# A new fixed order of all units in an attention backward kernel, placed with a longer latency for GpSimd's loads

## The chip, the cores and the metric

The kernel runs on one core of one Trainium2 chip. The metric is the device time of one execution in microseconds (us), lower is better. A profile shows a single execution.

## The reference, cut to what matters

```python
def _fwd_reference(q, k, v):                 # q: 32 x 32 x 4 x 128, k and v: 32 x 4 x 2048 x 128, bf16
    rep = Hq // Hkv                          # 8 query heads share one K/V head
    k = jnp.repeat(k, rep, axis=1)
    v = jnp.repeat(v, rep, axis=1)
    scores = jnp.einsum("bhqd,bhkd->bhqk", q, k) * D ** -0.5
    p = _softmax(scores, axis=-1)
    return jnp.einsum("bhqk,bhkd->bhqd", p, v)

def reference(q, k, v, grad_out):
    _out, _vjp = jax.vjp(_f, q, k, v)
    return (_out, *_vjp(grad_out))           # out, dq, dk, dv
```

There are 32 batches. A batch reads 4 MiB of K and V and writes 4 MiB of dK and dV; q, grad_out, out and dq are 32 KB each.

## The kernel before

The work of a batch is cut into units (a load, a group of eight transposes, a group of matmuls, a copy out of PSUM, a store). Five tables of constants decide everything else: `PLACE` and `SHIFT` give each unit a modelled time, and units are emitted in the order of these times; `ENGINE` and `SWAP` say which of ScalarE and VectorE empties a PSUM bank; `BANK` says which bank a unit gets. The order is fixed when the program is built. At run time each engine, and each DMA queue, takes its instructions in that order, and waits in front of one whose inputs or buffers are not ready.

```python
CAP = dict(q=4, k=8, v=4, ..., out=6)         # buffers: K tiles, V tiles, output tiles of 1 MiB, ...
PERIOD = 21.3
PLACE = dict(LQ=[-48.2636], LK=[-18.0693, -12.8344], LV=[-1.1987, -0.6906], ...)
SHIFT = {0: dict(...), 1: dict(...), ..., -1: dict(LQ=[49.6961], ...)}   # first and last batches

def plan(n_batches):
    # ... [cut]
            u.at = b * PERIOD + PLACE[name][i] + (SHIFT[special][name][i] if special in SHIFT else 0.0)
    # ... [cut]
    return sorted(order, key=lambda u: u.at), bank_of

def emit(u):
    # ... [cut]
        if name == "LQ":                                        # loads of q and grad_out, by GpSimd
            nc.gpsimd.dma_start(out=t["q"][:], in_=q_r[b])
            nc.gpsimd.dma_start(out=t["go"][:], in_=go_r[b])
        elif name in ("LK", "LV"):                              # 1 MiB: K or V of two heads, SyncE's queue
            # ... [cut]
                nc.sync.dma_start(out=whole[:, h], in_=src[b, g][:, h])
        elif name == "dop":                                     # grad_out / l, four GpSimd instructions
            # ... [cut]
                nc.gpsimd.tensor_scalar(out=t["dop"][r, h % 2, :], in0=t["go"][r, :], scalar1=t["rinv"][r, :],
                                        scalar2=None, op0=ALU.mult)
        elif name in ("DVs", "DKs"):                            # 1 MiB: dV or dK of two heads, SyncE's queue
            nc.sync.dma_start(out=(dv_r if name == "DVs" else dk_r)[b, g], in_=...)
```

Below, `31:LQ` is unit LQ of batch 31 (the last one), `0:DVs` the dV stores of batch 0. `DVh` and `DKh` are the half-size stores that the last batch uses instead of `DVs` and `DKs`.

Of the kernel before, what the change touches and what calls it, by code (L numbers as in the profile page):

```python
# [25 lines left out]
    LQ=[-48.2636], LK=[-18.0693, -12.8344], LV=[-1.1987, -0.6906], QT=[-8.9345], QTe=[-8.0517], KT=[3.2794, 2.2075,  # L26
    7.1287, 2.9279, -5.1008, 3.9474, 1.1495, 6.9051], KTe=[4.4019, 3.316, 7.8294, 3.9376, -3.2033, 4.9456, 1.413,
    8.201], VT=[10.6087, 11.8661, 12.1333, 11.0016, 22.6693, 19.1402, 21.0035, 29.0087], VTe=[11.5263, 13.3348,
    13.3464, 11.5339, 25.2055, 20.4113, 22.6987, 29.4066], S=[8.9164, 9.1359, 10.1684, 10.2742], MX=[9.726, 11.188],
    EX=[11.5488, 12.7509], L=[13.5403], dop=[14.9237], qp=[15.0712], rs=[22.4217], ET=[12.8706, 15.3517],  # L30
    ETe=[13.759, 16.5487], DT=[33.7403, 33.874], DTe=[35.0099, 35.0323], O=[16.8199, 17.0848, 17.1211, 17.3327],
    Oe=[17.6328], Os=[99.048], DQ=[49.0977, 49.2643, 51.8834, 52.2176], DQe=[52.222], DQs=[124.1403], DL=[18.4003],
    qfree=[30.7856], ofree=[101.8924], rfree=[76.464], DP=[19.5657, 19.5918, 32.7696, 32.8363], DS=[20.4794,
    33.0602], DV=[16.5613, 18.6959, 20.5469, 23.6255], DVe=[19.153, 18.3782, 19.7253, 19.9101, 21.6161, 22.5498,
    24.3354, 25.3252], DVs=[39.3395, 39.4734], DVh=[387.3484, 385.4967, 324.0755, 340.9939], DK=[27.2708, 29.0136,
    35.1757, 36.4881], DKe=[27.6123, 28.7618, 32.2561, 29.9139, 35.424, 36.2058, 37.166, 37.6438], DKs=[48.8067,
    50.1041], DKh=[309.6939, 275.5323, 368.4023, 239.5107], gfree=[72.3], dfree=[80.3411], vfree=[33.6388, 31.3008],
    efree=[38.0449], dsfree=[63.0633])
ENGINE = dict(
    QTe="A", KTe="DADAAAAA", VTe="ADDADAAD", ETe="AA", DTe="AD", Oe="D", DQe="A", DVe="AAADADAD", DKe="ADAAADAD")  # L40
SHIFT = {
    0: dict(
        LQ=[-644.2765], LK=[-547.0453, -364.6817], LV=[-242.4579, -342.359], QT=[-632.7948], QTe=[-537.9094],
        KT=[-526.8631, -326.7945, -226.1179, -229.4531, -211.8817, -445.3626, -187.0175, -311.721], KTe=[-449.298,
        -165.5918, -147.4492, -161.5852, -132.9361, -215.7495, -111.6072, -147.4306], VT=[-97.4249, -92.3852,
        -107.2125, -59.3954, -4.7301, -90.5139, -47.2652, -2.9351], VTe=[-60.891, -41.3598, -100.4245, -33.8442,
        -5.7782, -35.7373, -46.6873, -2.5874], S=[-133.3945, -128.0896, -116.6589, -105.6517], MX=[-103.1307,
        -96.1978], EX=[-80.1859, -76.7809], L=[-69.1857], dop=[-39.1633], qp=[-3.0986], rs=[-28.5145], ET=[-62.3285,
        -40.4913], ETe=[-61.4401, -37.8095], DT=[-2.4503, 3.8768], DTe=[-3.2726, 5.1407], O=[-34.6895, -34.5605,
        -32.5426, -26.7439], Oe=[-22.3532], Os=[-90.6858], DQ=[0.9913, 1.1827, -0.1837, -0.4072], DQe=[0.4358],  # L50
        DQs=[-25.8332], DL=[-23.0407], qfree=[3.6845], ofree=[-77.4158], rfree=[-47.2796], DP=[-15.6901, -15.0886,
        -0.2677, -0.1337], DS=[-9.2259, 0.0507], DV=[-20.5882, -20.1317, -17.8862, -7.8066], DVe=[-22.7759, -19.3155,
        -14.5522, -18.4952, -14.7281, -14.851, -6.2499, -2.6803], DVs=[-7.1188, -6.2006], DVh=[95.9489, -13.6628,
        190.2837, 256.3967], DK=[-2.3257, 0.2661, -0.196, 4.6202], DKe=[-1.4443, -2.8552, -2.3906, 0.6497, 4.8007,
        4.4534, 5.2752, 5.067], DKs=[2.5501, 6.7883], DKh=[92.5601, 315.3518, 14.3092, 206.3769], gfree=[-33.114],
        dfree=[12.6331], vfree=[2.3226, -3.4381], efree=[16.241], dsfree=[-14.3615]),
    1: dict(
        LQ=[-273.2258], LK=[-172.9572, -173.197], LV=[-143.8962, -84.7141], QT=[-102.2987], QTe=[-95.0311],
        KT=[-13.5143, -10.931, -12.2749, 1.5848, -41.1927, -6.8878, -4.2267, -0.3856], KTe=[-14.2854, -7.3948,
        -5.0963, 3.5831, -26.9748, -1.8969, 2.7732, 0.0956], VT=[-0.92, 9.5148, 7.5599, 0.4076, 9.5424, -1.3453,  # L60
        7.2294, 3.2881], VTe=[-1.2694, 8.8214, 8.208, 4.7262, 7.0746, -0.1221, 7.2436, 4.0334], S=[-0.4612, 0.1422,
        -0.8601, -0.7784], MX=[-0.0261, -0.3402], EX=[-0.3014, -1.4823], L=[2.9579], dop=[5.4261], qp=[8.1163],
        rs=[18.2432], ET=[4.2204, 4.2313], ETe=[5.5073, 3.7202], DT=[10.4883, 9.0141], DTe=[12.2528, 8.8384],
        O=[4.7696, 4.6756, 4.6399, 4.8799], Oe=[5.2421], Os=[-65.6303], DQ=[1.38, 2.4818, 0.5752, 0.4214],
        DQe=[0.8305], DQs=[-55.6573], DL=[6.6664], qfree=[-4.54], ofree=[-57.6955], rfree=[-31.2509], DP=[6.481,
        7.1462, 1.8519, 2.011], DS=[6.8437, 2.1623], DV=[6.1219, 4.2673, 4.013, 2.3696], DVe=[3.5646, 4.7633, 4.6339,
        3.2794, 4.2827, 2.5896, 2.6562, 2.5872], DVs=[-2.2225, -1.6614], DVh=[-48.0565, 92.0837, 212.991, 35.3116],
        DK=[1.4616, 2.399, 1.9843, 3.2316], DKe=[2.8105, 2.4108, 0.0521, 1.7291, 2.7773, 2.093, 4.3314, 3.6258],
        DKs=[-0.2539, 3.2382], DKh=[166.0226, -179.6575, -73.4159, 147.7363], gfree=[-20.4604], dfree=[-2.9502],
        vfree=[-0.986, 9.6916], efree=[9.973], dsfree=[-2.5173]),  # L70
    2: dict(
        LQ=[-226.2607], LK=[-125.0715, -101.8322], LV=[-0.0207, 5.1438], QT=[8.3657], QTe=[8.4261], KT=[-0.6224,
        0.899, -0.6109, 1.3692, -3.2051, 0.6568, -5.266, -0.6214], KTe=[-0.8606, 0.1636, 0.71, 0.4623, -3.8052,
        1.5449, -3.7401, 2.1648], VT=[4.6333, 1.8901, 0.9838, 3.0692, 0.7141, -0.2386, 5.2825, 2.8587], VTe=[6.9543,
        2.3385, 0.1001, 3.5582, -0.6809, -0.0455, 7.0247, 2.6881], S=[0.7118, 0.7725, 0.9176, 1.9061], MX=[1.3006,
        1.0295], EX=[2.6275, 2.1271], L=[1.7013], dop=[4.1629], qp=[6.121], rs=[26.8258], ET=[1.7596, 0.7913],
        ETe=[0.9226, 1.8347], DT=[0.0306, 1.0605], DTe=[-0.3559, 0.5948], O=[-0.6169, -0.689, 1.3759, 2.5991],
        Oe=[2.9753], Os=[-67.6709], DQ=[0.0477, 0.0266, 0.0798, 0.0503], DQe=[0.8654], DQs=[-29.5725], DL=[2.9999],
        qfree=[4.1668], ofree=[-15.8956], rfree=[8.5061], DP=[2.2626, 2.4079, -0.183, 0.2604], DS=[1.8788, 0.8895],
        DV=[3.9405, 2.0583, 1.9364, 0.8421], DVe=[2.3675, 2.5347, 1.8823, 1.7249, 0.973, 0.3188, 1.0135, 0.1142],  # L80
        DVs=[2.2247, 2.1669], DVh=[89.449, -133.5564, 149.9551, -67.7309], DK=[0.4886, 0.4113, 0.2255, -0.6123],
        DKe=[1.0637, 0.5283, -1.1784, 1.4927, 0.3966, -0.1425, -0.8541, -0.295], DKs=[0.0017, -0.7345],
        DKh=[-24.8477, -236.2928, 68.0068, -87.7762], gfree=[-8.276], dfree=[-24.2037], vfree=[7.272, 7.4296],
        efree=[0.4751], dsfree=[-3.0715]),
    -4: dict(
        LQ=[15.7312], LK=[9.1388, 3.5298], LV=[2.6948, 4.1417], QT=[4.5533], QTe=[5.4834], KT=[3.5433, 2.5662,
        -0.2541, 0.1587, 3.1776, -0.1333, -0.521, -6.2674], KTe=[2.8804, 1.5709, -0.1428, 0.5823, 2.6427, 0.1147,
        1.0893, -3.6722], VT=[0.4775, 1.6209, 0.0714, 0.8068, 1.8141, -4.6081, -1.7901, -1.974], VTe=[-0.3763,
        0.4613, -0.2881, 0.6884, 2.0307, -4.2152, -2.3562, -2.0356], S=[-0.7909, -0.605, -0.0342, 0.0555],
        MX=[1.4859, 0.26], EX=[0.4082, -0.1924], L=[0.2697], dop=[0.4758], qp=[1.2736], rs=[29.0407], ET=[1.3562,  # L90
        -1.1711], ETe=[1.0688, -1.0541], DT=[0.2943, 0.7101], DTe=[-0.2636, 0.009], O=[-1.5808, -0.9766, -0.8997,
        0.289], Oe=[0.9255], Os=[123.0701], DQ=[2.6734, 3.7048, 2.5956, 3.0928], DQe=[5.0872], DQs=[-3.9513],
# [48 lines left out]
        vfree=[366.8082, 177.2502], efree=[412.9433], dsfree=[391.0614])}  # L141
SWAP = {
    0: dict(
        KTe="-xx-x---", VTe="--x-x-x-", DTe="-x", DQe="x", DVe="x-xx----", DKe="xx--xx--"),
    1: dict(
        QTe="x", KTe="x-x-x-x-", VTe="-xxxx---", DTe="-x", DVe="-x--xx-x", DKe="xx--xxxx"),
    2: dict(
# [388 lines left out]
```

## Time and profile before

| | before |
|---|---|
| median of 3 executions | 694.3 us (693.08 to 694.78) |
| span of the profiled execution | 691.9 us |
| moved | 274.5 MB at a mean of 397 GB/s |
| PE busy, ScalarE busy | 90%, 87% |

These lines are from the page of the kernel before. The digits are the busy share, in tenths, of 40 equal slices of the span.

```profile
span 691.9 us, 28403 instructions
...
PE   5899999999999999999999999999999998998895
...
DMA  8999999999999999999999999999999999999958
...
DMA packets 75005, 274.47 MB, mean 397 GB/s; under 512 B 6272, under 2 KB 6272, under 8 KB 74880
```

The DMA engines are busy in nearly every slice, and so is PE. The transfers have slack at the end. These are the windows of the kernel before there (first the stretch; then the busy time of PE, of its weight loads, of VectorE, ScalarE and GpSimd, with instruction counts; then the granted TensorE clock, the DMA share and GB/s):

```profile
650.00:655.00 5.00, 2.54 (x45) 1.43 (x34) 1.68 (x5) 2.13 (x5) 3.33 (x7) 0.83 0.99 395
655.00:660.00 5.00, 5.00 (x71) 3.64 (x70) 4.18 (x4) 3.50 (x6) 0.00 (x0) 0.83 0.19 74
660.00:665.00 5.00, 4.14 (x69) 2.31 (x70) 4.19 (x5) 4.77 (x7) 0.00 (x0) 1.00 0.98 385
665.00:670.00 5.00, 4.89 (x125) 3.96 (x121) 4.74 (x10) 4.81 (x8) 1.02 (x2) 1.00 0.18 63
...
685.00:692.00 7.00, 0.91 (x48) 0.56 (x40) 0.06 (x1) 1.09 (x3) 1.06 (x2) 0.91 0.55 205
```

PE has a hole in 650 to 655, and the DMA engines have holes in 655 to 660 and 665 to 670. The timelines say why. PE (start, duration, instruction, idle time before it and what ended it), then GpSimd, of the kernel before:

```profile
650.26 0.62 PE L382 MATMUL psum<-ident,k_sb 128*128 128x128 bf16 x8
653.20 0.28 PE L371 MATMUL psum<-ident,q_sb 128*128 128x128 bf16 x1 [2.33 <-DMA q_sb<-in_q_dram]
...
653.84 1.03 PE L487 MATMUL psum<-dop_sb_102,e_sb 64*128 64x256 bf16 x8
```

```profile
647.52 0.59 POOL L357 DMA_DIRECT2D q_sb<-in_q_dram  x1
648.11 0.54 POOL L359 DMA_DIRECT2D go_sb<-in_grad_out_dram  x1
...
687.12 1.06 POOL L463 DMA_DIRECT2D out_dram<-dq_sb  x2 [10.94 <-ACT dq_sb L459]
```

GpSimd issues the last loads of q and grad_out at 647.5 and 648.1 us, behind the products of batch 30. PE waits 2.33 us for q, and the groups after the wait take 1.03 us instead of 0.61. The last dq stores are issued at 687.12 us.

This is the transfer rate from 25 to 65 us, in slices of one microsecond, of the kernel before:

```profile
GB/s 397 395 410 408 307 395 399 406 397 238 262 422 389 422 406 430 410 434 410 328 332 397 408 440 389 412 397 424 410 434 406 422 389 426 418 422 422 418 406 406
```

There are dips at 29, at 34 and 35, and at 44 and 45 us.

### The profile page before, as it was taken

Reading aid. Unit: us, or ns where it says so; the run is one execution under the profiler, and the core shown is the slowest. Engines: PE = TensorE matmul, PEld = TensorE weight load, DVE = VectorE, ACT = ScalarE, POOL = GpSimd, SP = SyncE. Lnnn points to the kernel's source line nnn. Section 1 sums busy time; section 2 is a strip of 40 time slices with the busy share of each in tenths; the row PEclk is TensorE's granted clock in tenths of the full one; section 3 lists DMA queues with packets and bytes.
Section 4 is the critical chain, followed back from the end, with each engine's and each line's share of the span. In section 5 each row is a group of like instructions: output and inputs, shape, how many; then the busy total and the mean of one; then the engine's idle time right before and its main releaser. Section 6 shows DMA issues by size and latency. Waiting matters only on the chain.

```text
span 691.9 us, 28403 instructions
## 1 busy us (share of the span) xinstructions
PE 625.0 (90%) x12352; PEld 468.6 (68%) x12352; DVE 556.6 (80%) x773; ACT 599.6 (87%) x924; POOL 203.2 (29%) x426
## 2 busy tenths in 40 slices
PE   5899999999999999999999999999999998998895
PEld 4677677777777777767767666676676776766563
DVE  2788888888889888888887878778787887889685
ACT  2889988899999999998889898888988998897685
POOL 2432311333322233331133321233312333213421
PEclk9999999999999999999999999999999999999999
DMA  8999999999999999999999999999999999999958
GB/s 340 394 391 415 415 413 411 413 413 416 414 416 416 414 415 411 387 410 412 411 399 410 411 409 412 406 397 401 399 406 408 402 406 402 411 391 392 364 211 302
DMA packets 75005, 274.47 MB, mean 397 GB/s; under 512 B 6272, under 2 KB 6272, under 8 KB 74880
## 3 DMA queue, kind: packets, MB, share of 16 engines
q1 hardware_dynamic: 70784, 268.45, 97.2%
q0 software_dynamic: 4096, 4.20, 1.8%
q8 instruction: 96, 1.57, 0.8%
q14 instruction: 29, 0.24, 0.1%
HBM read 136.31 MB, written 136.31 MB: 394 GB/s over the span
## 4 chain that ended last, share of the span: by engine, by line
DMA 41%; PE 26%; ACT 21%; issue 5%; DVE 3%; POOL 3%; ACTq 0%; POOLq 0%; DVEq 0%
DMA v_sb<-in_v_dram 37%; PE psum L382 15%; PE psum L487 7%; ACT dk_sb L493 6%; ACT dv_sb L493 5%; ACT e_sb L409 4%; DMA k_sb<-in_k_dram 3%; ACT vt_sb L347 3%; PE psum L452 2%; PE psum L393 2%; DMA go_sb<-in_grad_out_dram 2%; POOL dop_sb_103 L421 1%; ACT et_sb L347 1%; POOL dop_sb_102 L421 1%; ACT kt_sb L347 1%
## 5 line engine op out<-in xcount | busy, mean ns | idle before, releaser
L493 ACT CAST dv_sb<-psum 128x1024 bf16<-128x1024 f32 x155 | 151.5, 1018 | 33.3 <-PE psum L487 30.9
L493 ACT CAST dk_sb<-psum 128x1024 bf16<-128x1024 f32 x159 | 159.1, 1022 | 21.6 <-PE psum L487 21.1
L382 PE MATMUL psum<-ident,v_sb 128*128 128x128 bf16 x2048 | 150.2, 220 | 11.4 <-DMA v_sb<-in_v_dram 7.9
L382 PEld LDWEIGHTS <-v_sb 128*128 128x128 bf16 x2048 | 118.2, 98 | 51.0 <-issue 37.4
L382 PE MATMUL psum<-ident,k_sb 128*128 128x128 bf16 x2048 | 142.3, 221 | 1.3 <-ACT dv_sb L493 0.6
L382 PEld LDWEIGHTS <-k_sb 128*128 128x128 bf16 x2048 | 119.8, 99 | 15.7 <-issue 12.5
L493 DVE CAST dv_sb<-psum 128x1024 bf16<-128x1024 f32 x101 | 122.7, 1220 | 9.2 <-PE psum L487 7.9
L493 DVE CAST dk_sb<-psum 128x1024 bf16<-128x1024 f32 x97 | 116.1, 1220 | 16.2 <-DMA out_dram<-dv_sb 9.2
L347 ACT COPY kt_sb<-psum 128x512 f32<-128x512 f32 x187 | 106.7, 612 | 4.7 <-PE psum L382 4.7
L421 POOL TENSOR_SCALAR dop_sb_103<-go_sb,rinv 32x128 bf16<-32x128 bf16 x64 | 38.4, 600 | 227.5 <-DVE rinv L414 100.0
L421 POOL TENSOR_SCALAR dop_sb_102<-go_sb,rinv 32x128 bf16<-32x128 bf16 x64 | 38.4, 600 | 227.4 <-DVE rinv L414 114.1
L473 DVE SCALAR_TENSOR_TENSOR ds_sb<-psum,delta,e_sb 128x1024 bf16<-128x1024 f32 x64 | 81.9, 1279 | 16.7 <-ACT vt_sb L347 12.1
L347 ACT COPY vt_sb<-psum 128x512 f32<-128x512 f32 x137 | 80.5, 599 | 12.1 <-PE psum L382 11.8
L350 DVE COPY vt_sb<-psum 128x1024 bf16<-128x1024 bf16 x119 | 78.7, 680 | 1.0 <-PE psum L382 1.0
L487 PEld LDWEIGHTS <-e_sb 64*128 64x128 bf16 x1024 | 50.5, 94 | 37.3 <-issue 19.0
L409 ACT ACTIVATE e_sb<-psum,m 128x1024 bf16<-128x1024 f32 x64 | 70.9, 1116 | 2.7 <-DVE kt_sb L400 2.5
L350 DVE COPY kt_sb<-psum 128x1024 bf16<-128x1024 bf16 x69 | 47.1, 683 | 17.0 <-PE psum L382 16.8
L487 PEld LDWEIGHTS <-ds_sb 64*128 64x128 bf16 x1024 | 43.2, 94 | 24.8 <-issue 10.0
L441 PE MATMUL psum<-ident,e_sb 128*128 128x128 bf16 x512 | 38.8, 219 | 11.8 <-ACT dk_sb L493 10.5
L487 PE MATMUL psum<-dop_sb_103,e_sb 64*128 64x256 bf16 x512 | 46.0, 271 | 3.6 <-POOL dop_sb_103 L421 1.2
L487 PE MATMUL psum<-dop_sb_102,e_sb 64*128 64x256 bf16 x512 | 45.9, 273 | 3.6 <-ACT dv_sb L493 0.7
L400 DVE TENSOR_SCALAR_CACHE_REDUCE kt_sb<-psum 128x1024 bf16<-128x1024 f32 x32 | 39.2, 1224 | 9.1 <-PE psum L393 8.3
(83 smaller groups left out, 757.8 us busy)
## 6 DMA issues: line engine op xcount, KB each, us to landing
k_sb<-in_k_dram SPq DMA_DIRECT2D x62, 1024.0 KB, 18.6
v_sb<-in_v_dram SPq DMA_DIRECT2D x62, 1024.0 KB, 19.7
out_dram<-dv_sb SPq DMA_DIRECT2D x62, 1024.0 KB, 18.8
out_dram<-dk_sb SPq DMA_DIRECT2D x62, 1024.0 KB, 18.8
k_sb<-in_k_dram SPq DMA_DIRECT2D x4, 512.0 KB, 5.4
v_sb<-in_v_dram SPq DMA_DIRECT2D x4, 512.0 KB, 9.7
out_dram<-dv_sb SPq DMA_DIRECT2D x4, 512.0 KB, 5.6
out_dram<-dk_sb SPq DMA_DIRECT2D x4, 512.0 KB, 4.4
```

Of the source, the lines that this page charges most:

```text
L347: nc.scalar.copy(out=out.rearrange("p c d -> p (c d)").bitcast(FP32), in_=in_.rearrange("p c d -> p (c d)").bitcast(FP32))
L350: nc.vector.tensor_copy(out=out, in_=in_)
L382: nc.tensor.transpose(out=ps[:, j, :], in_=t[x, h][:, 8 * i + j, :], identity=ident[:])
L393: nc.tensor.matmul(t[name, i][r, QW * w:QW * w + QW], lhsT=t["qdt"][:, side, r], rhs=t[x, h, i][:, CPQ * w:CPQ * w + CPQ, :], start=True, ...
L400: nc.vector.tensor_scalar(out=spent, in0=t["S", i][:], scalar1=-scale, scalar2=t["m"][:] if i else None, op0=ALU.mult, op1=ALU.min, accum_ ...
L409: nc.scalar.activation(out=t["e"][:, 2 * QW * i:2 * QW * i + 2 * QW], in_=t["S", i][:], func=ACT.Exp, bias=t["m"][:], scale=scale, accum_o ...
L421: nc.gpsimd.tensor_scalar(out=t["dop"][r, h % 2, :], in0=t["go"][r, :], scalar1=t["rinv"][r, :], scalar2=None, op0=ALU.mult)
L441: nc.tensor.transpose(out=ps[:, j, :], in_=src[:, P * c:P * c + P], identity=ident[:])
L452: nc.tensor.matmul(t[name][r, 0:D], lhsT=t[xt, c // 8][:, c % 8, r], rhs=t[x, h][:, c, :], start=(c == 0), stop=(c == C - 1), tile_positio ...
L473: nc.vector.scalar_tensor_tensor(out=t["ds"][:, w], in0=t["DP", i][:], scalar=t["dl"][:], in1=t["e"][:, w], op0=ALU.subtract, op1=ALU.mult)
L487: nc.tensor.matmul(accs[g][:, 2 * P * j:2 * P * j + 2 * P], lhsT=t[lhs][r, P * c:P * c + P], rhs=t[rhs][r, :, :].rearrange("p h d -> p (h ...
L493: copy(out=t[name[:2], "out", g][:, :, CPQ * i:CPQ * i + CPQ, :], in_=t[name[:2], i][g][:].rearrange("p (c h d) -> p h c d", h=2, d=D))
```

## The change

The intent is a better fixed order, found with a model in which a load that GpSimd issues takes longer to arrive. All five tables are replaced; no line of code that emits an instruction is changed. Its core (of 277 lines of diff; everything cut is table entries):

```diff
 PLACE = dict(
-    LQ=[-48.2636], LK=[-18.0693, -12.8344], LV=[-1.1987, -0.6906], QT=[-8.9345], QTe=[-8.0517], KT=[3.2794, 2.2075,
+    LQ=[-47.936], LK=[-16.977, -14.467], LV=[3.599, 0.95], QT=[-7.484], QTe=[-6.947], KT=[2.869, 1.617, 7.32, 1.994,
 ... [cut]
 SHIFT = {
     0: dict(
-        LQ=[-644.2765], LK=[-547.0453, -364.6817], LV=[-242.4579, -342.359], QT=[-632.7948], QTe=[-537.9094],
+        LQ=[-769.808], LK=[-539.258, -428.322], LV=[-315.151, -320.416], QT=[-617.88], QTe=[-553.295], KT=[-481.834,
 ... [cut]
     -1: dict(
-        LQ=[49.6961], LK=[15.2382, -8.4226], LV=[48.932, 13.4729], QT=[23.4499], QTe=[23.5399], KT=[21.9244, 23.1949,
+        LQ=[53.318], LK=[12.855, 10.423], LV=[-0.474, 0.666], QT=[35.277], QTe=[36.759], KT=[27.228, 18.475, 11.67,
 ... [cut: the rest of PLACE and SHIFT, one entry of ENGINE, SWAP, BANK]
```

Both programs have the same 3,936 units, the same bytes and the same sizes of transfers. What moves, read from the order of instructions:

- Steady batches: the two V loads change places in SyncE's queue; PE's order is nearly the same.
- Tail, GpSimd: before, `29:dop 29:qp 25:DQs 30:dop 31:LQ 30:qp` (among others); after, `31:LQ` comes before `25:DQs 30:dop`. On PE the transposes of the last q come later in the order.
- Head, SyncE's queue: before, `... 2:LK 1:LV | 0:DVs 0:DVs 2:LV 3:LK 2:LV 3:LK`; after, `... 2:LK 1:LV 3:LK | 0:DVs 3:LK 0:DVs 2:LV 2:LV`. One K load of batch 3 passes both first stores, the other passes one of them.

## The prediction

> What bounds the kernel now. The page's DMA row is at 9 tenths in nearly every slice: 274.5 MB at a mean of 397 GB/s over 691.9 us. By windows: the DMA engines are full (share 1.0) from about 5 us to 655 us; the rate is 412 to 416 GB/s from 100 to 260 us and 399 to 410 after. Up to about 278 us the chain of waits runs through PE and ScalarE pieces, with a period near 20.3 us a batch; from 278 to 640 us it runs through loads of v_sb, about 21.1 us apart. Wherever the transfers are the limit, reordering the engines' work gains nothing, because bytes, transfer sizes and the steady queue order stay as they are (the listing of instruction order shows only that the two V loads of a batch change places).
>
> The end is different. From 640 to 692 us the chain has no bulk load. The DMA share falls to 0.19 in 655-660, 0.18 in 665-670, 0.76 in 670-675 and 0.55 in 685-692: some 12.5 us of empty DMA time. In the same stretch PE is busy 90% or more except in 650-655 (2.54 of 5 us), where ScalarE and VectorE fall to about 2 us too. The timeline shows why: GpSimd issues the last batch's q and grad_out loads only at 647.5 and 648.1, behind the four products of batch 30 (644.8-647.5). grad_out takes 5.46 us in the chain; PE waits for q_sb until 653.2 (idle 2.33 us) and for grad_out 0.32 us on weight load; all PE work behind stands in order. The next three PE groups then take 1.03 us instead of 0.61 (granted clock 0.83 in 650-660).
>
> What the change does. No operation is added or removed: 3,936 units in both; ScalarE gets 856 units instead of 859, VectorE 648 instead of 645; a steady batch has 27 and 20 in both. The function bodies are the same. On GpSimd the last q/grad_out load moves before batch 30's products, to just after batch 29's (about 622-629 us), over 15 us ahead of its use. So the PE stall (2.3 + 0.3 us) and the slow clock after it (3 x 0.42 us) go: about 4 us, all on the chain, since the following stores wait for that PE work. The Trainium skill ("TensorE: Matmul & The Clock Gate", "Part 1") says an idle PE falls to a slower clock and must be busy about 3.4 us to regain it; the trace agrees in kind (1.03 against 0.61 us).
> Smaller things: the first K transpose no longer shares a PSUM bank with the q transpose (0.35 us, hidden behind the transfers); the last dq store is no longer ahead of the previous batch's (-0.5 us), but one transpose of dS stands closer to its use (+0.4). Head: one or two more K loads ahead of the first stores, under 1 us.
>
> Estimate: 694.3 - 4.3 = 690.0 us; range 683.5 to 694.5. Floor, from the rates: 9.2 MB moved after 655 us at the 363 GB/s that stores alone reach would end near 681 us, so over 2% (below 680.4) needs a faster middle too. Chances: faster 0.05, same 0.93, slower 0.02.
>
> Right if: no PE wait for q_sb near 650; granted clock 1.0 in 650-660; DMA share in 655-660 rises from 0.19 to about 0.6; the last dv stores start about 4 us earlier; the stretch 100-600 us keeps its rate within 1%.
>
> Wrong if: the steady rate shifts between the 416 and the 404 GB/s regimes at another time (12 us at most), or the new tail order makes a new stall (PSUM banks are all reassigned), or the end was held by the store rate alone.

## The result, and the profile after

A ratio is the mean time of one kernel's fast runs over that of the other's of the same rounds, so it is not quite the ratio of the medians quoted.

| run of the changed kernel | median (range), us | before, same rounds | ratio (95% interval) |
|---|---|---|---|
| first | 692.02 (690.35 to 695.77) | 694.34 | 0.9979 (0.995 to 1.0009) |
| `after_again` | 692.27 (690.99 to 695.29) | 694.78 | 0.9969 (0.9945 to 0.9992) |
| `after_3` | 692.14 (691.42 to 694.93) | 695.26 | 0.9962 (0.9945 to 0.9979) |
| `after_4` | 692.11 (691.4 to 695.02) | 694.66 | 0.9965 (0.9949 to 0.9982) |

The mean of the four ratios is 0.9969: the change saves about 2.2 us of 694.6, half of the 4.3 us predicted. The time is inside the predicted range, which says little, since the range (683.5 to 694.5 us) also holds the 694.3 us of the kernel before; and "within 2%" came true.

These windows of the changed kernel answer to those shown of before:

```profile
650.00:655.00 5.00, 5.00 (x79) 3.46 (x72) 4.75 (x5) 4.82 (x8) 0.00 (x0) 1.00 0.96 386
655.00:660.00 5.00, 3.05 (x64) 1.70 (x65) 3.35 (x6) 3.65 (x6) 0.00 (x0) 1.00 0.90 361
660.00:665.00 5.00, 5.00 (x123) 4.14 (x109) 4.69 (x8) 5.00 (x9) 1.19 (x2) 1.00 0.11 39
665.00:670.00 5.00, 4.02 (x109) 3.15 (x107) 4.37 (x9) 3.35 (x6) 4.26 (x11) 1.00 0.84 329
...
685.00:692.00 7.00, 0.00 (x0) 0.00 (x0) 0.00 (x0) 0.00 (x0) 0.00 (x0) 0.60 0.02 6
```

PE's hole of 650 to 655 is gone (5.00 of 5 us) and the clock is full. The DMA hole in 655 to 660 is filled (0.19 became 0.90). But PE has a new hole in 655 to 660, and one DMA hole remains, in 660 to 665. PE's and GpSimd's timelines of the changed kernel:

```profile
650.81 0.22 PE L361 MATMUL psum<-ident,q_sb 128*128 128x128 bf16 x1
...
656.48 0.62 PE L372 MATMUL psum<-ident,v_sb 128*128 128x128 bf16 x8 [1.13 <-DMA v_sb<-in_v_dram]
```

```profile
626.63 0.60 POOL L347 DMA_DIRECT2D q_sb<-in_q_dram  x1
...
682.08 0.54 POOL L453 DMA_DIRECT2D out_dram<-dq_sb  x1 [4.17 <-DVE dq_sb L451]
```

The last q load is issued 20.9 us earlier than before and nobody waits for it. PE now runs into the next thing that is not there, the V load of batch 31. (This profile is of the fastest of the six executions, 690.35 us.)

To compare tails of executions that reach the end at different times, take the moment at which PE starts on V of batch 30 as zero (639.81 us before, 637.71 us after). Then the last dq store has been issued at 48.4 us before (687.12 + 1.06 - 639.81) and at 44.9 us after: the last store is issued 3.5 us sooner, close to the predicted 4.3 (0.5 us of this is that one dq store is issued there, and no longer two). But the span ends at 52.1 and 50.9 us: only 1.2 us sooner. What lies between is the landing of that store. The transfers of the last 10.5 us, before and then after (what, queue, how many, size, median us from issue to landing):

```profile
out_dram<-dq_sb POOLq DMA_DIRECT2D x2, 32.0 KB, 2.7
```

```profile
out_dram<-dq_sb POOLq DMA_DIRECT2D x1, 32.0 KB, 4.8
```

The last dq store takes 2.1 us longer to land. The transfer rate in the last 12 us of the span, in slices of 0.3 us, shows what it waits for, before and then after:

```profile
GB/s 362 403 362 382 376 403 362 430 355 150 362 369 382 375 362 410 382 362 382 410 375 355 389 389 403 375 396 389 212 205 82 48 14 0 0 0 0 0 0 0
```

```profile
GB/s 375 410 355 280 410 396 314 396 212 328 376 369 396 369 410 369 369 375 389 396 382 396 362 219 89 48 41 27 27 27 20 27 27 14 0 0 0 0 0 0
```

Before, the rate falls from 389 to nothing within 1.5 us, and it does so when the last dq store has been issued (688.18 us, slice 28): compute and transfers end together. After, the rate breaks down shortly after the last dq store has been issued (683.5 us, slice 23, against 682.6), but then runs on at 20 to 27 GB/s for 2 us. That is one engine of 16 (410 / 16 = 26). The compute is done, 15 engines are done, and the end waits for the last one. Most of what this engine still moves is not the dq store: of the 28 packets from 684.7 to 686.8 us, 26 belong to SyncE's queue, whose last transfers are the large dK stores, and 2 to GpSimd's. A lone engine, or two, also fills the gaps further up (the trace does not name the engines, so whether it is always the same one is not known). The rate from 640 to 692 us, in slices of 1.3 us, before and then after:

```profile
GB/s 410 410 419 419 388 384 394 410 408 421 408 229 134 43 28 189 400 403 400 240 38 25 35 25 353 394 406 378 331 362 377 377 334 372 384 378 392 181 6 0
```

```profile
GB/s 429 406 425 372 347 331 395 416 403 395 343 403 425 416 318 95 32 38 22 54 394 397 400 381 299 339 350 375 370 372 325 377 392 249 33 24 0 0 0 0
```

Before has two gaps, after has one, and within each the rate stays between 22 and 43 GB/s for 3 to 5 us. PE's new wait of 1.13 us does not come from such a gap: the V load of batch 31 lands at 656.43 us, 19.5 us after its issue (the median of the large V loads is 19.6 us), and the gap begins only at 658 us. And PE has slack there. In the profile of `after_again` the clock is halved for 3.41 us right after the start on V of batch 30. PE still reaches V of batch 31 after 18.7 us (18.8 us in the changed kernel's first profile), now without a recorded wait, and from V of batch 30 to the end it is 50.8 us, against 50.9.

The rest of the difference lies before the tail: in the profiled executions, V of batch 30 is there 2.1 us sooner. One profile cannot tell whether that is the change or chance (the four profiles of the unaltered changed kernel have it at 637.71, 641.29, 638.86 and 642.14 us); the experiments must. In windows of 80 or 100 us, the rates from 100 to 600 us are the same within 1%. In the head, the changed kernel (25 to 65 us, slices of 1 us) has no dips at 29 and 34, and a new one at 54 to 57:

```profile
GB/s 410 406 406 397 371 397 371 406 430 410 426 393 414 426 414 426 406 430 426 401 414 406 426 414 406 381 406 414 414 324 277 352 395 406 414 418 426 397 414 397
```

### The profile page after: what moved, and what is told of

Same layout as the page of the kernel before. It is cut to its first block, busy times and chain, and to the rows that moved or that the text cites. A ratio compares the mean times of both kernels' runs of the same rounds, so it can differ in the third digit from the quotient of the medians.

```text
span 688.6 us, 28403 instructions
## 1 busy us (share of the span) xinstructions
PE 620.1 (90%) x12352; PEld 467.1 (68%) x12352; DVE 558.3 (81%) x776; ACT 604.4 (88%) x921; POOL 208.8 (30%) x426
## 2 busy tenths in 40 slices
DMA packets 75005, 274.47 MB, mean 399 GB/s; under 512 B 6272, under 2 KB 6272, under 8 KB 74880
## 4 chain that ended last, share of the span: by engine, by line
DMA 55%; PE 22%; ACT 13%; issue 5%; POOL 3%; DVE 2%; SPq 0%; POOLq 0%; DVEq 0%; ACTq 0%
DMA v_sb<-in_v_dram 52%; PE psum L372 10%; PE psum L477 6%; ACT dk_sb L483 4%; ACT dv_sb L483 4%; PE psum L431 3%; DMA out_dram<-dv_sb 2%; ACT e_sb L399 2%; PE psum L442 2%; ACT vt_sb L337 2%; POOL dop_sb_103 L411 1%; PE psum L383 1%; DVE kt_sb L390 1%; ACT kt_sb L337 1%; DMA go_sb<-in_grad_out_dram 1%
## 5 line engine op out<-in xcount | busy, mean ns | idle before, releaser
L372 PE MATMUL psum<-ident,v_sb 128*128 128x128 bf16 x2048 | 147.4, 220 | 16.8 <-DMA v_sb<-in_v_dram 15.3
L372 PEld LDWEIGHTS <-k_sb 128*128 128x128 bf16 x2048 | 121.4, 99 | 27.1 <-issue 24.3
L337 ACT COPY kt_sb<-psum 128x512 f32<-128x512 f32 x190 | 110.3, 595 | 6.6 <-PE psum L372 5.1
L337 ACT COPY vt_sb<-psum 128x512 f32<-128x512 f32 x131 | 75.5, 599 | 17.6 <-PE psum L372 16.6
L340 DVE COPY vt_sb<-psum 128x1024 bf16<-128x1024 bf16 x125 | 82.9, 681 | 2.9 <-PE psum L372 2.6
L477 PEld LDWEIGHTS <-e_sb 64*128 64x128 bf16 x1024 | 50.0, 93 | 36.3 <-issue 19.6
L340 DVE COPY kt_sb<-psum 128x1024 bf16<-128x1024 bf16 x66 | 44.9, 685 | 18.8 <-PE psum L372 18.8
L477 PE MATMUL psum<-dop_sb_103,e_sb 64*128 64x256 bf16 x512 | 45.2, 270 | 4.1 <-POOL dop_sb_103 L411 1.6
L477 PE MATMUL psum<-dop_sb_102,e_sb 64*128 64x256 bf16 x512 | 44.9, 270 | 3.2 <-ACT dv_sb L483 0.7
L390 DVE TENSOR_SCALAR_CACHE_REDUCE kt_sb<-psum,m 128x1024 bf16<-128x1024 f32 x32 | 41.1, 1284 | 6.5 <-DVE kt_sb L390 3.9
## 6 DMA issues: line engine op xcount, KB each, us to landing
k_sb<-in_k_dram SPq DMA_DIRECT2D x62, 1024.0 KB, 18.7
v_sb<-in_v_dram SPq DMA_DIRECT2D x62, 1024.0 KB, 19.6
out_dram<-dk_sb SPq DMA_DIRECT2D x62, 1024.0 KB, 18.8
```

Source lines behind the costliest of these rows:

```text
L337: nc.scalar.copy(out=out.rearrange("p c d -> p (c d)").bitcast(FP32), in_=in_.rearrange("p c d -> p (c d)").bitcast(FP32))
L340: nc.vector.tensor_copy(out=out, in_=in_)
L372: nc.tensor.transpose(out=ps[:, j, :], in_=t[x, h][:, 8 * i + j, :], identity=ident[:])
L390: nc.vector.tensor_scalar(out=spent, in0=t["S", i][:], scalar1=-scale, scalar2=t["m"][:] if i else None, op0=ALU.mult, op1=ALU.min, accum_ ...
L477: nc.tensor.matmul(accs[g][:, 2 * P * j:2 * P * j + 2 * P], lhsT=t[lhs][r, P * c:P * c + P], rhs=t[rhs][r, :, :].rearrange("p h d -> p (h ...
```

## The experiments

All kernels gave correct results. Edits move a unit by giving it another modelled time; the hook is the same in all of them but `after_small_sp`:

```diff
+MOVED = {(31, 'LQ'): 650.0}
 ...
+            u.at = MOVED.get(u.key, u.at)
     return sorted(order, key=lambda u: u.at), bank_of
```

The theory at the start was that of the prediction: the early q and grad_out load takes a stall away and the whole stall comes off the time. Its rivals: the tail is held by the transfers, so that an engine that is sooner ends in another wait; or the gain comes from the head.

### Is the gain real: the changed kernel again

> The changed kernel once more, unaltered, to settle its size beside the others on one chip. The forecast's theory (the last q/grad_out load alone is worth about 4 us): 0.994 of before. Rival theory (the gain is capped near the end, because the last V load and the lagging transfers become the limit): 0.996 to 0.999 of before, 691 to 693.5 us.

> The changed kernel a third time, for comparison on one chip: 0.997 of before, as in the two runs so far (0.9979 and 0.9969).

Measured: 0.9969 and 0.9962 (table above). The gain is real, and it is 2 to 2.6 us, not 4.3. The slower executions of the changed kernel tend to have a lower mean clock: of the 24 in its four runs, 10 have 0.996 or more and take 691.6 us in the mean, the other 14 take 693.4 us. This goes with its larger spread; that it causes it was not tested.

### The early load alone, in the kernel before

```diff
+MOVED = {(31, 'LQ'): 650.0}        # kernel before: 31:LQ ahead of 26:Os, 25:DQs and 30:dop
```

> Before with one change: the last batch's q/grad_out load is issued ahead of batch 30's products on GpSimd. Forecast's theory: the PE wait of 2.3 us and the slow clock after it go, and the span falls by about 4 us (0.994). Rival: the PE wait goes as well and the last compute ends about 3 to 4 us earlier, but PE then waits for the last V load (1 us or more near 655 to 658), and the last small store lands later after its issue (over 5 us instead of 4), so only 1 to 2.5 us are gained (0.9965 to 0.9985).

> The kernel before with the last q/grad_out load early, again, since its first ratio (0.9984) and that of both edits (0.9956) came from two chips and differ by more than the head edit alone (1.0005) can explain. If the first ratio holds: 0.998 to 0.999. If the early load is worth more: 0.996 to 0.997.

> The kernel before with only the early last q and grad_out load, a third time, for the same rounds as the others. Both theories: 0.998, plus or minus 0.001, as twice before.

Measured: 693.71, 693.93 and 693.56 us; ratios 0.9984 (0.9966 to 1.0001), 0.9981 (0.9968 to 0.9995) and 0.9988 (0.997 to 1.0005). The mean, 0.9984, is 1.1 us. Two of the three intervals reach 1; it is the repetition that makes a gain likely. PE's and GpSimd's timelines of `before_lq_early`:

```profile
650.37 0.22 PE L373 MATMUL psum<-ident,q_sb 128*128 128x128 bf16 x1
...
658.37 0.62 PE L384 MATMUL psum<-ident,v_sb 128*128 128x128 bf16 x8 [1.32 <-DMA v_sb<-in_v_dram]
```

```profile
684.33 1.07 POOL L465 DMA_DIRECT2D out_dram<-dq_sb  x2 [10.94 <-ACT dq_sb L461]
```

The stall and the slow clock after it are gone, as predicted. PE then meets V of batch 31 and waits 1.32 us for it. Counted from the start on V of batch 30 (639.47 us), the last dq store has been issued after 45.9 us, 2.4 us sooner than in the kernel before, and the span (690.8 us) ends after 51.3 us, 0.8 us sooner. The last dq stores take longer to land here as well, 4.4 us instead of 2.7, with the lone engine at 20 to 27 GB/s in the last slices:

```profile
out_dram<-dq_sb POOLq DMA_DIRECT2D x2, 32.0 KB, 4.4
```

So of a stall of 2.6 us and 1.3 us of slow clock, PE gives back 1.3 us in a new wait, and the last landing keeps 1.6 us of the 2.4 that remain. The profiles of the other runs agree: from V of batch 30 to the end it is 52.1, 53.1 and 51.5 us in the three kernels of before's order with the late load (mean 52.2), 51.3 to 51.5 us in the six with the early load, and 50.8 to 51.1 us in the four unaltered runs of the changed kernel (mean 50.9). (In the profile with 53.1 us PE also waits 1.04 us for grad_out.) The one with 51.5 us, `head_loads_2`, has the wait for q as well, but not the slow clock:

```profile
652.50 0.23 PE L373 MATMUL psum<-ident,q_sb 128*128 128x128 bf16 x1 [2.48 <-DMA q_sb<-in_q_dram]
...
653.07 0.61 PE L489 MATMUL psum<-dop_sb,e_sb 64*128 64x256 bf16 x8
```

The granted clock is 1.00 there from 640 to 684 us, and although PE lost 2.48 us, the end comes within 0.2 us of the kernels with the early load. In this one profile the wait itself is nearly all hidden. The early load is the prediction's claim by itself, and it is worth a quarter of what was claimed.

### The load put late again, in the changed kernel

```diff
+MOVED = {(31, 'LQ'): 669.5}        # changed kernel: 31:LQ back behind 30:dop
```

> After with the last q/grad_out load put back behind batch 30's products. Forecast's theory: PE waits for q_sb again, and it is about 4 us slower than after (1.006 of after), that is slower than before or equal to it. Rival: the wait comes back but 1 to 2.5 us of it hide, since the V load's wait of 1.1 us goes and the last store lands sooner: 1.0015 to 1.0035 of after.

Measured: 692.48 us, 0.9969 (0.995 to 0.9988): the same as the changed kernel of the same rounds (0.9969). So neither theory of the expectation held. In this profile the load is issued at 647.09 us, behind the products of batch 30 again, and PE has no wait for q. In the changed kernel PE's order puts other work of batch 30 ahead of the q transposes: they start 14.1 us after V of batch 30 (655.33 - 641.26), where the kernel before was ready for them after 11.1 us (650.87 - 639.81). And the products of batch 30 come sooner after V of batch 30, so that the load is issued 5.8 us after it instead of 7.7. The early position of the load, which the prediction named as the cause, is therefore not what removes the stall in the changed kernel; the order around it does that already.

### The next wait taken away: V of batch 31 earlier

```diff
+MOVED = {(31, 'LV', 1): 657.0, (31, 'LV', 0): 657.1}   # changed kernel: both V loads ahead of 29:DVs
```

> After with the two V loads of the last batch issued ahead of the two dV stores of batch 29. If the engines' chain through the V load limits the end: PE's wait at 656 (1.1 us, 1.8 us with the weight load) goes, and the time falls by 1.5 us or more (0.998 or less of after). If the transfers' total work limits it: the wait goes, the compute ends earlier, and the time stays within 0.7 us of after.

Measured: 694.58 us, 0.9993 (0.9974 to 1.0012), some 2 us slower than the changed kernel. The wait for V is gone, and another one came, as the waits of this kernel from 650 to 665 us show:

```profile
DVE dk_sb L485 <- DMA out_dram<-dv_sb: 4.6, 1, 4.6
```

The stores that were passed give their output tiles back later, so the copies of dK of batch 30 wait for a tile (there are six). PE is busy only 1.35 us of 655 to 660, and the clock falls to 0.66 in 660 to 665. To take this wait away too, dK of batch 30 went into K buffers that nobody needs any more at the end:

```diff
+                    if (b, name) == (30, "DK"):
+                        t[name, "out", g] = k_pool.tile([P, 2, C, D], BF16, name="k_sb")
+                        continue
```

> After with the last batch's V loads ahead of batch 29's dV stores, as tried before, and batch 30's dK output tiles in two K buffers that are free by then, so that they don't wait for those stores. If the wait for an output tile was what made the first try slower: the 4.6 us wait of VectorE for a dv store goes, the V load lands near 651, PE is busy over 4.5 us in 655-660, and the time is 1.5 to 3 us below after. If the transfers' total work limits the end: the waits go and the last small store lands later after its issue, within 0.7 us of after.

Measured: 692.04 us, 0.9975 (0.9957 to 0.9993). Both waits are gone and PE is busy 5.00 us of 655 to 660, yet this is no faster than the changed kernel (0.9969). From V of batch 30 on the last dq store has been issued after 44.4 us (44.9 in the changed kernel), and the span ends after 50.5 us (50.9), again with 4.8 us for the last landing. A wait of 1.1 us was taken out of PE, and 0.4 us reached the end of this one profile. (PE began this tail at a lower clock, 0.77 in 640 to 645, so the profile does not say how much of the rest that cost.) In the six executions, taking away this wait of PE gained nothing.

### The head alone, and both edits, in the kernel before

```diff
+MOVED = {(3, 'LK', 0): 32.2007, (3, 'LK', 1): 32.2107}                      # head: 3:LK ahead of 0:DVs
+MOVED = {(3, 'LK', 0): 32.2007, (3, 'LK', 1): 32.2107, (31, 'LQ'): 650.0}   # both
```

> Before with the two K loads of batch 3 issued ahead of the first dV stores, as the changed kernel nearly does, and nothing else. Theory (half of the gain comes from the head): the transfer rate of 25 to 60 us rises from 391-393 to about 400 GB/s, PE's first long wait for V starts about 1 us sooner (276.5 instead of 277.5), and the time falls by 0.8 to 1.3 us (0.998 to 0.999 of before). Rival (the head is made up for by the full queue later): no change, within 0.4 us.

> The kernel before with only the head edit (both K loads of batch 3 ahead of batch 0's dv stores), a repeat (first time 1.0005, interval 0.998 to 1.003). Theory A (the head edit fills transfer time that the tail can only use when the last q and grad_out load is early as well): 1.000 again, within 0.0015. Rival B (the head edit is worth 1 to 2 us by itself, and the first reading was spread): 0.997 to 0.9985.

> Before with both edits: the K loads of batch 3 earlier in the head and the last q/grad_out load earlier at the end. If these two are what the whole change is worth: 0.9969 of before, as the changed kernel, 2 to 2.5 us less. If the gain of the changed kernel lies in the order of the other units: 0.9985, no better than the early q load alone.

> Both edits again on the same chip as the early load alone and the changed kernel. If the edits add: within 0.5 us of the early load alone. If the head loads help only beside the early load: 1.5 us below it, and below the changed kernel.

> Both edits together, a third time. Both theories: 0.9956, plus or minus 0.001. Under rival B the three of these runs add up (head alone times early load alone gives both); under theory A both is better than their product by 0.002 or more.

| kernel before, with | ratios to before | mean |
|---|---|---|
| the head edit | 1.0005 (0.9984 to 1.0026), 0.9999 (0.9981 to 1.0017) | 1.0002 |
| the early load | 0.9984, 0.9981, 0.9988 (intervals above) | 0.9984 |
| both | 0.9956 (0.9943 to 0.9969), 0.9956 (0.9944 to 0.9969), 0.9963 (0.9946 to 0.9979) | 0.9958 |

Both edits together save 2.9 us (medians 691.33, 692.11 and 691.83 us). These two moves of three units get all that the new order of 3,936 units gets, and a little more, though the intervals overlap. The head edit alone saves nothing that can be measured, and beside the early load it saves 1.8 us. The two do not add up, in the same rounds as well (0.9999, 0.9988 and 0.9963); the excess over the product, 0.0028 or 1.9 us, is hardly more than the half-widths of the intervals. Why the head edit should need the early load is not shown, and stays open.

The recorded mean clock of each execution gives a hint. All 35 executions of the kernel before with the early load (alone or with the head edit) have a mean clock of 0.996 or more. Of the 55 of the kernel before in the same rounds only 10 do, and of the 12 with the head edit alone only one. That one is their fastest, 692.14 us, near the 691.8 us that both edits take in the mean; the other 11 take 694.6 us in the mean. So the head edit alone may lose its gain to slow clock like that after the wait for q (0.66 in 655 to 660 us in the profile of `before_head_loads`), which the early load avoids. In the kernel before itself the two kinds of executions do not differ (694.6 and 694.7 us), and no experiment tested this.

What the head edit does in the transfers can be seen. SyncE's queue is in order: a store whose data is not ready keeps back the loads behind it. If the K loads of batch 3 stand behind the first stores, the loads already under way run out before dV of batch 0 is ready (issued at 28.68 us), and the rate dips. The price comes later: the rate dips between 54 and 60 us. To put one number on it, the table adds up what each slice of 1 us from 25 to 65 us lacks to 410 GB/s, in units of 410 GB/s times 1 us; slices above 410 count against it.

| head order | transfer time lost from 25 to 65 us, each profile |
|---|---|
| stores first, kernel before and early load | 1.4, 1.6, 1.9, 1.8 us |
| K loads first, head edit and both | 1.7, 0.9, 0.7, 1.5, 0.5 us |
| changed kernel, and with its load late | 0.8, 0.7, 1.2, 1.7, 0.6 us |
| changed kernel with the head set back (next experiment) | 2.3, 2.6 us |

The mean goes from 1.7 to 1.1 us in the kernel before: a gain of 0.6 us, with the second dip as the uncertain part.

### The head set back, in the changed kernel

```diff
+MOVED = {(3, 'LK', 0): 50.8, (3, 'LK', 1): 51.95}   # changed kernel: 3:LK behind 0:DVs, next to 2:LV, as before
```

> The changed kernel with the head's transfer order set back (batch 3's K loads behind batch 0's dv stores and next to batch 2's V loads, as in the kernel before). If the head order carries a part of the change's gain (1 to 2 us), this is slower than the unaltered changed kernel: 0.9985 to 1.000 instead of 0.9969. If the head order is worth nothing here: 0.996 to 0.998.

> The changed kernel with the head's transfer order set back, a repeat (first time 0.9995). If the head order carries the change's gain: 0.998 to 1.000 again, and slower than the unaltered changed kernel of the same rounds by 1 us or more. If the first reading was spread: 0.997, equal to the unaltered one.

> The changed kernel unaltered, in the same rounds as head_back_2. All theories: 0.9966 plus or minus 0.001, as the mean of the three earlier runs.

Measured: 694.33 us, 0.9995 (0.9977 to 1.0013), and 694.31 us, 1.0002 (0.9983 to 1.0021); the unaltered changed kernel 692.11 us, 0.9965 (0.9949 to 0.9982). Without the head order the gain is gone, although the tail is as short as in the changed kernel (50.8 us from V of batch 30 on in both profiles). The rate from 25 to 65 us of `after_head_back`, and SyncE's longest wait up to 40 us in it and in the changed kernel:

```profile
GB/s 414 389 414 369 125 301 397 393 397 360 184 266 377 422 410 422 426 418 422 401 348 373 430 408 416 410 401 410 430 410 430 416 395 416 424 406 422 414 406 397
```

```profile
SPq L494 <- DVE dv_sb L485: 15.6, 1, 15.6
```

```profile
SPq L492 <- DVE dv_sb L483: 12.6, 1, 12.6
```

With the stores first, the queue stands still for 15.6 us in front of the first dV store (12.6 us with one more K load ahead of it), and the rate falls to 125 GB/s at 29 us and 184 at 35 us. That is deeper than in the kernel before (307 and 238); the new order has its first dV a little later (the store is issued at 29.42 us instead of 28.68). The table above puts the loss at 1.4 us more than with the changed kernel's own head. The times say 0.0030 or 2.1 us against the mean of the changed kernel's four runs, and 0.0037 or 2.6 us in the rounds that hold both. So the new compute order needs its new head order, and by itself is worth nothing that can be measured.

### Two tests of what slows the transfers

The one engine that finishes last in each gap suggested a cause to remove. The Trainium skill ("DMA: Bandwidth & Descriptors", section "Latency and other measured facts") says that engines 7 and 15 are usually slower, and offers as a best guess, not certain, contention from the descriptor rings of GpSimd-issued transfers. And its section "Why a DMA increments its semaphore by 16 and not by 1" says that the number of engines of a transfer is the largest number up to 16 that divides the outer dimension of both its sides, so that, by an estimate from that rule, 120 partitions would use 15 engines.

```diff
+        small = nc.sync if 3 <= b <= 27 else nc.gpsimd      # q, grad_out, out, dq of batches 3 to 27 by SyncE
-            nc.gpsimd.dma_start(out=t["q"][:], in_=q_r[b])
+            small.dma_start(out=t["q"][:], in_=q_r[b])
 ... [cut: grad_out, out and dq likewise; out stores placed 35 and dq stores 50 earlier in the order]
```

> After with the small loads and stores of batches 3 to 27 issued by SyncE on the queue of the large ones, instead of by GpSimd, stores earlier in the order so that they land in time. The Trainium skill's page on DMA guesses that transfers issued by GpSimd slow two of the sixteen engines. If that is the one that goes on alone in every gap and holds the V loads up: PE's waits for V in 300 to 600 us shrink, the rate in 300 to 600 rises from 405 to 410 GB/s or more, 5 us or more are gained. If the transfers' total work is the limit whoever issues them: within 2 us of after.

Measured: 695.5 us, 1.0002 (0.9982 to 1.0021), slower than the changed kernel of the same rounds (0.9962). With the small transfers on the bulk queue the rate was 397 to 398 GB/s from 180 to 500 us, where the changed kernel has 407 to 411 (and 408 against 402 from 500 to 640 us). So the edit is no remedy. It is not a clean test of the rings either: GpSimd still issues the small transfers of the first and last batches, and the transfers that moved came in smaller packets (19,072 packets under 512 B, 6,272 in the changed kernel), which may slow them by itself.

```diff
-                nc.sync.dma_start(out=whole[:, h], in_=src[b, g][:, h])
+                for r in (slice(0, 120), slice(120, 128)) if name == "LK" and g == 0 and b % 2 == 1 else [slice(0, 128)]:
+                    nc.sync.dma_start(out=whole[r, h], in_=src[b, g][r, h])
```

> After with the first K load of every odd batch cut in two transfers, partitions 0 to 119 and 120 to 127, which by the Trainium skill's page on DMA run on the engines 0 to 14 and 0 to 7: engine 15 is spared 1 transfer in 16. In every gap of the transfers one engine alone goes on for 3 to 5 us at about 25 GB/s. If that is engine 15, and it holds up the others: the lone stretch shrinks below 1.5 us and the time falls by 2 us or more. If it is one of 0 to 7: 2 to 5 us slower. If another, or if the lag does not matter: within 1 us of after.

Measured: 738.91 us, 1.0639 (1.0611 to 1.0667). Splitting 16 of the 1 MiB loads into 120 and 8 partitions costs 47 us, 2.9 us for each. In the stretches looked at (60 to 140 and 300 to 380 us) the rate dips to between 190 and 330 GB/s for 3 to 9 us at a time, with the DMA engines busy nearly throughout. The gap near the end is still there (slices of 47 to 50 and then 25 GB/s), and the last dq store still takes 4.9 us to land. How the data was spread over the engines was not settled, so the run refutes the edit as a remedy and does not explain the lone engine.

## Why the prediction was right or wrong

**What bounds the kernel: right.** From 278 us on the chain is mostly V loads, and the rates from 100 to 600 us stayed within 1%.

**What would show each step: all seen.** No PE wait for q near 650; clock 1.00 in 650 to 660; DMA share of 655 to 660 up from 0.19 (to 0.90, where 0.6 was predicted); the last dV stores 3.2 us earlier, counted from V of batch 30 (675.02 - 639.81 = 35.2 us before, 669.70 - 637.71 = 32.0 us after; those of batch 30 start 4.4 us earlier, 15.2 instead of 19.6). And still the time fell by half of what was predicted. The markers all lie upstream of the end; none of them asked what the end waits for.

**The step that failed: "about 4 us, all on the chain, since the following stores wait for that PE work".** The stall and slow clock do go, and the last store is issued 3.5 us sooner in the changed kernel, 2.4 us with the early load alone. What reaches the time is 1.1 us with the early load alone (1.1, 1.3 and 0.8 us in its three runs). So the stall was not "all on the chain": PE met the V load of batch 31 (1.0 to 1.5 us of new wait in most profiles), and the last dq store took longer to land (4.4 to 4.8 us instead of 2.7), because one DMA engine was still at work. The compute and the transfers ended together before; taking time from one of them only shows the other. The prediction had a neighbour of this among its risks ("the end was held by the store rate alone") but gave it no share of the estimate. How the stall comes about was right; the term of the sum, 4.3 us, measures 1.1. The slow clock that the term counts with the stall is not certain either: of the three profiles with the stall, two have it and `head_loads_2` has not.

**The cause that it named: wrong for the changed kernel.** It ascribed the gain to the early position of the last q and grad_out load. With the load put late again the changed kernel is as fast.

**"Head: one or two more K loads ahead of the first stores, under 1 us": the size was about right as a difference to the kernel before, the role was wrong.** The lost transfer time of the head falls by 0.7 us (means of the table, 1.7 and 1.0). But with its compute order alone, the changed kernel loses 0.8 us more there than the kernel before (2.42 against 1.65), and without the head order no gain can be measured.

**The sum.** For the changed kernel, 1.3 us of tail (52.2 - 50.9, means of the profiles) and 0.7 us of head make 2.0 us; measured are 2.2 us. That this fits is partly luck. The same sum gives 0.8 + 0.6 = 1.4 us for both edits in the kernel before, where 2.9 are measured, and 1.4 - 0.8 = 0.6 us for the changed kernel with the head set back, where 0.1 is measured; and the 52.2 is the mean of three profiles between 51.5 and 53.1.

**The Trainium skill, as the prediction used it:** "TensorE: Matmul & The Clock Gate", "Part 1", says that an idle PE drops to a slower clock. The trace shows it: 1.03 us instead of 0.61 after the 2.33 us wait, with a granted clock of 0.50 for 3.41 us, and groups of 1.04 and 1.05 us after waits of 1.47 and 2.46 us in `after_v_first`. But the length of a wait alone does not decide here. After waits of 1.1 to 1.3 us for V no group slowed down; after waits near 2 us the clock fell in `after_again` (1.98 us) and not in `after_3` (1.99 us); and in `head_loads_2` it stayed full after 2.48 us. The same page puts the idle window at about 3.4 us, and no wait shown here is that long.

**What stays open:** why the head edit alone saves nothing in the kernel before while it saves 1.8 us beside the early load (the clock is a suspect, not tested); and why one DMA engine finishes after the others, by 3 to 5 us in the gaps and by 2 us at the end of the changed kernel (with its load late too) and of the kernels with the early load, but hardly at the end of the kernel before.

## What to carry to other kernels

When a stall sits in the last stage, ask what else ends there before booking it in full: count from one common event to the last issue and to the end of the span, and look at how long the last transfer takes to land. An in-order transfer queue is a resource of its own: a store whose data is not ready, placed ahead of loads that could start, lets the DMA engines run empty (here the rate dipped to 307 GB/s and less), and moving it is one line; whether that pays has to be measured, since here it did so only beside other changes. Of a wholesale reordering, test the pieces alone and set each one back; here two moves of three units did as much as the five new tables. And look at the granted clock of every execution, not of the profiled one alone.

## What the Trainium skill lacked or had wrong

- "DMA: Bandwidth & Descriptors", "Why a DMA increments its semaphore by 16 and not by 1", says that the engines finish independently and only the full count means that all data has landed. It gives no size for the spread. Here one engine, or two, works on alone for 3 to 5 us when the transfers run dry (22 to 43 GB/s of 410), and for 2 us at the end of the changed kernel.
- The same page, "Anatomy of one DMA", fits a GpSimd-issued transfer as 2.0 us plus its bytes over 436 GB/s, which makes an estimate of 2.1 us for 32 KB. Under the load of this kernel the 32 KB loads and stores took 5.4 to 6.0 us (medians), and the last dq stores 2.7 to 4.8 us. The page says elsewhere that the fixed part grows with the load on HBM; a figure for a loaded queue is missing.
- The same page, "Bandwidth", lists loads only. Here the last stores, with no loads beside them, moved 361 to 366 GB/s in the kernel before (675 to 685 us), where mixed traffic moved 404 to 416 (100 to 580 us).
- The same page gives contention with GpSimd's rings as a best guess for slow engines. Taking GpSimd out of the small transfers of 25 of 32 batches brought no gain (1.0002 against 0.9962). Since their packets became smaller as well, this does not decide the guess.
- "Perfetto Trace Analysis", "Roofline", takes about 120% of 358 GB/s as the practical ceiling of a single core. This agrees: 397 GB/s over the span (111%), 416 in the best windows (116%).
- No page says what a split into 120 and 8 partitions costs beside full streams: 2.9 us for each 1 MiB load here.
